# S4D mixing kernel: transposes of x in queues of their own, measured durations in the planner, shared buffers and one merged product

## The chip, the cores and the metric

The kernel runs on one core of a Trainium2 chip. The metric is the time of one execution on the device in microseconds (us), the median of several runs. The core has five engines with programs of their own: TensorE (PE in the profile, with its weight loads as PEld), VectorE (DVE), ScalarE (ACT), GpSimd (POOL) and SyncE (SP), which issues nearly all DMAs here.

## The reference

Sequence length L is 2048, the model width D 640, the hidden width 1728, and the state size N 128. All data is fp32.

```python
x = A_u                                                       # [1, 2048, 640]
g = sigmoid((x * gate_w).sum(-1, keepdims=True))
# A: S4D. A = -exp(log_A_real) + i A_imag, dt = exp(log_dt), C = (C_real + i C_imag) dt
P = exp((A * dt[:, None])[:, :, None] * pos)                  # [640, 128, 2048], pos = 0..2047
K = 2 * einsum("dn,dnl->dl", C, P).real                       # one filter of 2048 taps per channel
a = irfft(rfft(x^T, 2 L) * rfft(K, 2 L))[..., :L]^T + x * D_skip
# B: feed-forward
b = relu(x @ w1) @ w2
return g * a + (1 - g) * b
```

## The kernel before, in words

Three kinds of work share the core, and a planner interleaves them.

*Feed-forward* (`feed_forward`). The hidden width is cut into 14 tiles of 128, done in three passes of 5, 5 and 4 tiles; each matmul operand is split into a high and a low fp32r part (names ending in `h` and `l`), and three products stand for one. Pass 0 goes through eight blocks `g` of 256 rows. Block g is loaded (`load_x`, tile `xu`), transposed on PE (`trans`, in three thirds of two, two and one chunk of 128 columns, into a PSUM bank: `pk` for every block but the first), copied by ACT as the high part and subtracted by DVE as the low part (both into the tile `xx`, which has room for two blocks, ring `xhl`), and stored to DRAM for the later passes (`xt`). `hidden` multiplies it with w1, ACT and DVE make the split relu (`hh`, `hl`), and `sums` multiplies with w2 into partial sums `q` that are stored in DRAM (`part`) and loaded again by the next pass. Passes 1 and 2 take blocks in pairs (`wide`, 512 columns). All of these PE steps stand in one in-order queue, `ff`, with the transposes of block g + 1 between the hidden products of block g.

*Generation of the taps* (`params`, `ssm`). After a chain of parameter steps on DVE, 40 units of 16 channels each are made: `phases` (PE into bank `pg`, ACT takes the whole turns into `cs`, DVE the fraction into `sn`), `exponents` (PE into `px` and `pe`, ACT takes exponentials `mg`, 64 coarse ones per channel, and `me`, 32 fine ones, then sine and cosine in place in `sn` and `cs`), `factors` (five DVE products; the first half of the 64 columns of `sn` and `cs` is the fine table, the second half the coarse one), and per two units `taps` (256 small matmuls into bank `pk`, the same ring as the transposes of x, then a DVE transpose, tile `kt`, and stores to DRAM, `kd`).

*Convolution* (`conv`). Five blocks of 128 channels go through a two-step transform (`stage1` for filter and input, `stage2` with the products of the spectra, `inv2`, `relay`, `inv1`). All its matmuls write PSUM tiles `pc` of two banks each from the ring `psc` of three. `inv1` works in two halves `j` and two parts `q`: two 128x512 products in the first bank of a tile, then four ACT multiplications with the gate into `yo`, which are joined with the partial sums of pass 1 or stored for pass 2.

*The planner.* Nothing is written in loops over engines. Every step is a `Task` with an engine, a queue, a duration, dependencies, buffers that it takes and uses, and a rank; `Plan.run` simulates the engines greedily in time (the lowest rank among the steps that are ready, each queue in order) and issues the instructions in the order so found, which is then the order of each engine's program. `LAG`, `CHANGE` (extra time when an engine changes mode: `f` full matmuls, `c` and `c1` convolution, `t` taps), `FETCH` and the DMA rate are its model of the chip; they carry no wait into the program but decide the order. A DMA step has a size `kb`, and the planner lets all DMAs run one after the other at 270 KB/us (230 in the first 12 us):

```python
if t.kb:
    dma = max(dma, start + min(t.dur, 0.62) + 0.5) + t.kb / (230 if start < 12 else 270)
    t.end = max(dma, start + t.dur) + 1.1
```

The line in the profile for nearly all instructions is L314, that of the helper `Pinned`, so groups are told apart by tiles.

Of the kernel before, what the change touches and what calls it, by code (L numbers as in the profile page):

```python
# [10 lines left out]
F32 = mybir.dt.float32  # L11
# [43 lines left out]
S2P = 2  # L55
RLR = 2
S4A = 0
POOLED = 0
PA = 3
PL = 2.5  # L60
YO = 5
# [80 lines left out]
class Plan:  # L142
# [5 lines left out]
    FETCH = 2.4  # L148
    BUSY = 2.6
    SLACK = .8  # L150
    BURST, GATHER, PATIENCE = ('c', 'c1'), 2, 3

    def __init__(self):
# [68 lines left out]
    def run(self):  # L222
# [3 lines left out]
        while True:  # L226
# [39 lines left out]
                break  # L266
            _, e, t, start = best
            change = self.CHANGE.get(e, 0) if t.mode is not None and mode.get(e) not in (None, t.mode) else 0
            if e == 'PE' and t.mode != 'f':
                since = start + t.dur  # L270
            if t.mode is not None:
# [16 lines left out]
                self.free[e] += 0.25 * min(max(self.free['POOL'] - start, 0), t.dur)  # L288
            t.end = self.free[e] + t.lag
            if t.kb:  # L290
                dma = max(dma, start + min(t.dur, 0.62) + 0.5) + t.kb / (230 if start < 12 else 270)
                t.end = max(dma, start + t.dur) + 1.1
            for b in (*t.take, *t.use):
                b.left -= 1
                b.free = max(b.free, t.end)
# [49 lines left out]
class Kernel:  # L345
# [30 lines left out]
    def feed_forward(self):  # L376
# [109 lines left out]
        def trans(g, third, src):  # L486
            s_, ld = src
            bank = ('pk', 'px', 'pg')[0 if g else third]
            b_ = tok(bank)
            if third == 0:  # L490
                xtok[0, g] = tok('xhl')
            x_ = xtok[0, g]
            k0, kn = 2 * third, min(2, NT - 2 * third)

            def pe():
                ps = self.psg.tile([128, 2 if bank == 'pk' else 4, 256], F32, name=bank)
                ps = st['xb', g, third] = ps[:, :2]
# [13 lines left out]
            a = A('PE', 'ff', 0.22 * kn, pe, [ld], take=[b_], use=[s_], mode='f')  # L511
            b = A('ACT', 'ff', 0.12 + 0.2 * kn, high, [a], take=[x_] if third == 0 else (),
                  use=[b_] if third == 0 else [b_, x_], rank=0)
            c = A('DVE', 'ff', 0.08 + 0.27 * kn, low, [b], use=[b_, x_], rank=0)
            X.setdefault((0, g), []).extend((b, c))
            self.x_read.append(a)

            def store():
                for l, x in enumerate(st['x', g]):
                    D_.dma_start(sc['xt'][g][l], x.bitcast(F32))  # L520
            if third == 2:
                if g:
# [88 lines left out]
        def wide(p, P, f):  # L611
# [34 lines left out]
            ts = [A('PE', 'ff', 0.69, pe(k), [*wt, *xd_], take=() if k else [b_], use=[w_, *xs_] + ([b_] if k else []),  # L646
                    mode='f', n=3) for k in range(NT)]
            a = A('ACT', 'ff', 0.52, high, [*ts, *(self.zs if p == 1 and f > 1 else ())], take=[h_], use=[b_], rank=0)
            b = A('DVE', 'ff', 0.62, low, [a], use=[b_, h_], rank=0)
# [141 lines left out]
        for p, n in enumerate(PARTS):  # L791
# [3 lines left out]
            for k, g in enumerate(order):  # L795
# [28 lines left out]
                if not last:  # L824
                    es = [sums(p, g, j, q_, qld) for j in range(4)]

                    def store(p=p, g=g):
                        D_.dma_start(sc['part'][p % 2][g], st['q', g])
                    done[p, g] = A('SP', 'st', 0.62, store, es, use=[q_], kb=640, rank=6, late=True)
                    continue  # L830
                if k % 2 == 0 and k < 6:
                    paced = [x for i in order[k + 2:k + 4] for x in X[p, i]]
# [179 lines left out]
    def ssm(self, C=16):  # L1012
# [52 lines left out]
        def phases(c):  # L1065
            p_, s_ = tok('pg'), tok('sc')
            rd, r_ = rows[c]

            def pe():
                p = self.psg.tile([128, 4, 256], F32, name="pg")  # L1070
                pf = p.rearrange("p d j -> p (d j)")
                st['pg'] = pf.rearrange("p (d j) -> p d j", j=64)
                for h in range(2):
                    x = slice(h * 512, h * 512 + 512)
                    self.E.matmul(pf[:, x], R[c], self.tg[:, x], start=True, stop=True)

            def whole():
                st['sc', c] = [st['gp'].tile([128, C, 64], F32, name=k, bufs=5) for k in ("sn", "cs")]
                S.copy(I(st['sc', c][1]), st['pg'])
            a = visit[c, 1] = A('PE', None, 0.5, pe, [rd, opened, *self.tg_done], take=[p_], use=[r_], rank=GPR, mode='f')  # L1080
            b = acts[c, 0] = A('ACT', None, 0.97, whole, [a], take=[s_], use=[p_], rank=2)
            d = A('DVE', 'g1', 1.14, lambda: V.tensor_sub(st['sc', c][0], st['pg'], I(st['sc', c][1])), [b],
                  use=[p_, s_], rank=G1R)
            e = A('DVE', 'g1', 0.62, lambda: V.tensor_scalar(I(st['sc', c][1]), I(st['sc', c][0]), 0x7fffffff, None,
                                                             op0=ALU.bitwise_and), [d], use=[s_], rank=G1R, port=True)
            tasks[c] = dict(s=s_, abs=e)

        def exponents(c):
# [13 lines left out]
            def exps(k):  # L1102
# [8 lines left out]
            a = visit[c, 2] = A('PE', None, 0.7, pe, [rd, opened, *self.tg_done], take=[p_], use=[r_], rank=GPR, mode='f')  # L1111
# [10 lines left out]
        def factors(c):  # L1122
# [3 lines left out]
            def part(k):  # L1126
                def go():
# [5 lines left out]
                    elif k == 1:  # L1133
                        V.tensor_mul(st['G', c][:, :, 32:], mg[:, :, 32:], sn[:, :, 32:])
                    elif k == 2:
                        m = mg.rearrange("p d (h j) -> p d h j", h=2)
                        V.tensor_mul(m, m, cs[:, :, None, 32:].to_broadcast([128, C, 2, 32]))
                    elif k == 3:
                        V.tensor_mul(cs[:, :, :32], me, cs[:, :, :32])
                    else:  # L1140
                        (P if POOLED else V).tensor_mul(sn[:, :, :32], me, sn[:, :, :32])
                return go
            (ex, me), (sn, cs) = w['exps'], w['trig']
            fs = []
            for k, dep in enumerate(((ex, sn), (ex, sn), (ex, cs), (me, cs), (me, sn))):
                if k == 4 and POOLED:
                    fs.append(A('POOL', 'g2', 1.5, part(k), dep, use=[w['s'], w['m']]))
                    continue
                fs.append(A('DVE', 'g4', 1.2 if k == 2 else 0.62, part(k), dep, take=[g_] if k == 0 else (),
                            use=[w['s'], w['m']] + ([g_] if k == 1 else []), rank=G4R, port=True))  # L1150
            w.update(G=g_, f=fs)

# [1 line left out]
        def taps(p):  # L1154
# [23 lines left out]
            a = visit[p, 0] = A('PE', None, 2.0, pe, [*w[0]['f'], *w[1]['f']], take=[b_], use=us, rank=GTR, mode='t', n=128)  # L1178
# [32 lines left out]
    def conv(self, C=128):  # L1211
# [182 lines left out]
        def inv1(i, j, dep):  # L1394
            last = i == n - 1
            for q in range(2):
                b_, b0 = tok('psc'), j * 8 + q * 4
                ns = min(max(2 * sum(c <= i for c in CG) - b0, 0), 4)
                y_ = tok('yo') if ns or not last else None
                g_, first = None, False  # L1400
# [4 lines left out]
                def pe(q=q, b0=b0):  # L1405
                    py = st['p4', i, b0] = self.psc.tile([128, 2, 4, C], F32, name="pc")
                    for h in range(2):
                        self.E.matmul(py[h * 64:h * 64 + 64, 0].rearrange("p b c -> p (b c)"), st['tw'],
                                      st['K', i][:, h * 4 + b0 // 4], start=True, stop=True)

                def copy(q=q, b0=b0, ns=ns, y_=y_, first=first):
# [4 lines left out]
                    x = st['p4', i, b0][:, 0].rearrange("p b c -> p (b c)").rearrange("p (c b) -> p b c", b=4)  # L1416
# [124 lines left out]
```

## Time and profile before

| | before |
|---|---|
| median of 3 runs | 644.29 us (642.56 to 644.78) |
| profiled execution | 642.35 us |
| its span, first to last instruction | 640.6 us |
| PE, PEld busy | 617.3, 503.0 us |
| DVE, ACT, POOL busy | 508.5, 402.1, 93.9 us |
| DMA | 107.78 MB, mean 168 GB/s |
| granted TensorE clock | 1.00 |

The profile is of one execution. A stretch in which PE is busy all the time is one that PE bounds, if its work is needed there; a wait names the instruction that stood still and what released it. An engine's idle time costs nothing where another engine sets the pace.

### The profile page before, as it was taken

To read this page: it belongs to the slowest core of one execution; us is meant where nothing else is said; L and a number is where in the kernel's file an instruction comes from. 1 tells how busy PE (TensorE), PEld (TensorE's weight loads), DVE (VectorE), ACT (ScalarE), POOL (GpSimd) and SP (SyncE) were. 2 spreads that over 40 slices of the span, in tenths; PEclk is the share of its full clock that TensorE was granted. 3 is DMA by queue.
4 is the path that set the end of the run, shared out by engine and by line. 5 is a ranking of instruction groups with operands and counts; after the bars stand their busy time and mean duration, and the time that the engine had idled before them with its cause. 6 is when DMAs were issued, how large, how long until landed. Compare 5 with 4: busy or idle time off the path is not lost.

```text
span 640.6 us, 19212 instructions
## 1 busy us (share of the span) xinstructions
PE 617.3 (96%) x8236; PEld 503.0 (79%) x8236; DVE 508.5 (79%) x818; ACT 402.1 (63%) x603; POOL 93.9 (15%) x134
## 2 busy tenths in 40 slices
PE   7989999899999899999999999999999999999897
PEld 6989998798898798898898898665565556756577
DVE  4889936989999999998999999768579753966542
ACT  5557439999999988988978985113443424432550
POOL 0000000000000000000000000024151531713633
PEclk9999999999999999999999999999999999999999
DMA  9974774333456734373454225794406558156355
GB/s 256 326 236 147 221 229 165 105 125 112 136 167 210 255 122 144 122 242 117 129 198 154 79 80 176 258 315 132 144 3 215 185 164 263 53 158 188 102 166 133
DMA packets 76176, 107.78 MB, mean 168 GB/s; under 512 B 7610, under 2 KB 58682, under 8 KB 75195
## 3 DMA queue, kind: packets, MB, share of 16 engines
q1 hardware_dynamic: 75930, 106.14, 53.2%
q8 instruction: 65, 1.06, 0.7%
q10 hardware_dynamic: 160, 0.41, 0.3%
q14 instruction: 21, 0.16, 0.1%
HBM read 67.47 MB, written 44.30 MB: 174 GB/s over the span
## 4 chain that ended last, share of the span: by engine, by line
PE 56%; DVE 5%; DMA 2%; ACT 2%; issue 1%; SPq 1%; DVEq 0%; ACTq 0%
PE pf L314 35%; PE pc L314 13%; PE pk L314 4%; DVE ku L314 3%; PE pg L314 2%; PE px L314 2%; DMA part<-q 1%; ACT ku L314 1%; PE pe L314 1%; DMA out_dram<-yo 1%; SPq L314 1%; DVE sn L314 1%; ACT cs L314 0%; DVE q L314 0%; ACT q L314 0%
## 5 line engine op out<-in xcount | busy, mean ns | idle before, releaser
L314 PE MATMUL pf<-xx,w1h 128*128 128x256 f32 (+1 forms) x760 | 184.2, 339 | 0.4 <-DVE xx L314 0.3
L314 PEld LDWEIGHTS pf<-xx,w1h 128*128 128x128 f32 x760 | 125.2, 189 | 22.8 <-issue 7.3
L314 PE MATMUL pf<-xx,w1l 128*128 128x512 f32 (+1 forms) x340 | 115.7, 340 | 0.0
L314 PE MATMUL pf<-w2h,hh 128*128 128x320 f32 x288 | 89.7, 315 | 2.4 <-DVE hl L314 1.5
L314 PE MATMUL pf<-w2l,hh 128*128 128x320 f32 x288 | 87.8, 309 | 0.0
L314 ACT COPY ku<-pc 128x512 f32<-128x512 f32 (+1 forms) x60 | 43.8, 761 | 68.2 <-PE pc L314 56.7
L314 PE MATMUL pf<-w2h,hl 128*128 128x320 f32 x256 | 73.3, 312 | 0.0
L314 PEld LDWEIGHTS pf<-xx,w1l 128*128 128x128 f32 x340 | 64.3, 189 | 7.6 <-DVE w1l L314 0.2
L314 POOL TENSOR_TENSOR kt<-kt,dsk 128x8 f32<-128x8 f32 x20 | 10.3, 515 | 392.7 <-DVE kt L314 377.8
L314 POOL TENSOR_TENSOR ku<-ku 128x256 f32<-128x256 f32 x80 | 56.2, 737 | 55.3 <-DVE ku L314 49.1
L314 DVE TENSOR_TENSOR ku<-pc,ku 128x512 f32<-128x512 f32 x80 | 52.6, 684 | 12.5 <-ACT ku L314 11.3
L314 DVE STREAM_TRANSPOSE ku<-pc 128x512 f32<-128x512 f32 x80 | 50.2, 683 | 13.7 <-PE pc L314 13.7
L314 PEld LDWEIGHTS pf<-w2h,hh 128*128 128x128 f32 x288 | 54.1, 188 | 7.7 <-issue 3.7
L314 DVE TENSOR_TENSOR sn<-pg,cs 128x1024 f32<-128x1024 f32 x40 | 48.7, 1217 | 7.5 <-ACT cs L314 7.5
L314 PEld LDWEIGHTS pf<-w2l,hh 128*128 128x128 f32 x288 | 54.1, 188 | 0.6
L314 ACT ACT_TABLE_LOAD x42 | 53.9, 1283 | 0.7
L314 ACT CAST cs<-pg 128x1024 int32<-128x1024 f32 x40 | 40.3, 1008 | 21.2 <-PE pg L314 21.0
L314 DVE TENSOR_TENSOR mg<-mg,cs 128x1024 f32<-128x1024 f32 x40 | 48.9, 1222 | 1.3
L314 PEld LDWEIGHTS pf<-w2h,hl 128*128 128x128 f32 x256 | 46.4, 188 | 3.5 <-issue 2.9
L314 PE MATMUL pc<-ku,tm 64*32 64x256 f32 x1280 | 42.2, 392 | 3.6 <-DVE ku L314 2.4
L314 ACT ACTIVATE cs<-cs,half_pi 128x1024 f32<-128x1024 f32 x40 | 45.6, 1140 | 0.0
L314 ACT ACTIVATE hh<-pf 128x512 fp32r<-128x512 f32 (+1 forms) x40 | 20.5, 513 | 39.4 <-PE pf L314 39.4
(170 smaller groups left out, 1232.5 us busy)
## 6 DMA issues: line engine op xcount, KB each, us to landing
xx<-xt SPq DMA_DIRECT2D x24, 640.0 KB, 6.8
xt<-xx SPq DMA_DIRECT2D x16, 640.0 KB, 3.9
part<-q SPq DMA_DIRECT2D x16, 640.0 KB, 3.4
q<-part SPq DMA_DIRECT2D x16, 640.0 KB, 5.3
ws<-in_B_w_dram SPq DMA_DIRECT2D x20, 320.0 KB, 5.5
kd<-kt SPq DMA_DIRECT2D x80, 64.0 KB, 1.8
ub<-in_A_u_dram SPq DMA_DIRECT2D x10, 512.0 KB, 4.7
xu<-ub SPq DMA_DIRECT2D x5, 1024.0 KB, 6.2
```

The source lines that it names most:

```text
L314: self._last = self._tc.keep_in_program_order(f(*a, **k))
```

## The change

It has five parts, all in one file.

- `trans`: the PE, ACT and DVE steps of x's transposes stand in queues `xp` of their own in place of `ff`, on PE at rank 4.5 (the rank of `ff` is 5; the lower goes first).
- `phases`, `factors`, `taps`: sine and cosine of a unit are two halves of one tile `sc`, and the two fine products with `me` become one DVE instruction over both (with `me` broadcast). The unused variant on POOL is deleted.
- `inv1`: the two parts `q` of a half share one PSUM tile, one bank each; the tile is freed after the second part's ACT copies.
- `Plan.run`: DMA steps have a rate by queue, a step of several DMAs is modelled as several, and the latencies are 1.15 and 1.27 us. A change of PE to or from taps costs half as much.
- Durations: `wide` 0.69 to 0.681 us, `phases` 0.5 to 0.46, `exponents` 0.7 to 0.69, `taps` 2.0 to 1.83, the store of partial sums from 640 to 310 KB.

```diff
+    RATE = dict(x=330, q=287, st=320, yq=200, y4=260, mx=297, cu=215, kd=231, ub=401, xt=485, rows=697, prm=215, tab=340, tab0=171)
...
+            if e == 'PE' and 't' in (t.mode, mode.get(e)):
+                change /= 2
...
             if t.kb:
-                dma = max(dma, start + min(t.dur, 0.62) + 0.5) + t.kb / (230 if start < 12 else 270)
-                t.end = max(dma, start + t.dur) + 1.1
+                m = max(1, round(t.dur / 0.625))
+                for j in range(m):
+                    dma = max(dma, start + 0.62 * j + 1.15) + t.kb / m / self.RATE.get(t.q, 250)
+                t.end = max(dma, start + t.dur) + 1.27
...
-            a = A('PE', 'ff', 0.22 * kn, pe, [ld], take=[b_], use=[s_], mode='f')
-            b = A('ACT', 'ff', 0.12 + 0.2 * kn, high, [a], take=[x_] if third == 0 else (),
+            a = A('PE', 'xp', 0.22 * kn, pe, [ld], take=[b_], use=[s_], rank=4.5, mode='f')
+            b = A('ACT', 'xp', 0.12 + 0.2 * kn, high, [a], take=[x_] if third == 0 else (),
                   use=[b_] if third == 0 else [b_, x_], rank=0)
-            c = A('DVE', 'ff', 0.08 + 0.27 * kn, low, [b], use=[b_, x_], rank=0)
+            c = A('DVE', 'xp', 0.08 + 0.27 * kn, low, [b], use=[b_, x_], rank=0)
...
-                    done[p, g] = A('SP', 'st', 0.62, store, es, use=[q_], kb=640, rank=6, late=True)
+                    done[p, g] = A('SP', 'st', 0.62, store, es, use=[q_], kb=310, rank=6, late=True)
...
-                st['sc', c] = [st['gp'].tile([128, C, 64], F32, name=k, bufs=5) for k in ("sn", "cs")]
+                t = st['tr', c] = st['gp'].tile([128, 2, C, 64], F32, name="sc", bufs=5)
+                st['sc', c] = [t[:, k] for k in range(2)]
...
-                    elif k == 3:
-                        V.tensor_mul(cs[:, :, :32], me, cs[:, :, :32])
                     else:
-                        (P if POOLED else V).tensor_mul(sn[:, :, :32], me, sn[:, :, :32])
+                        t = st.pop(('tr', c))[:, :, :, :32]
+                        V.tensor_mul(t, me[:, None].to_broadcast([128, 2, C, 32]), t)
...
-                fs.append(A('DVE', 'g4', 1.2 if k == 2 else 0.62, part(k), dep, take=[g_] if k == 0 else (),
+                fs.append(A('DVE', 'g4', 1.2 if k > 1 else 0.62, part(k), dep, take=[g_] if k == 0 else (),
...
-                b_, b0 = tok('psc'), j * 8 + q * 4
+                b0 = j * 8 + q * 4
+                b_ = b_ if q else tok('psc')
...
-                    py = st['p4', i, b0] = self.psc.tile([128, 2, 4, C], F32, name="pc")
+                    if not q:
+                        st['p4', i, j] = self.psc.tile([128, 2, 4, C], F32, name="pc")
+                    py = st['p4', i, j]
                     for h in range(2):
-                        self.E.matmul(py[h * 64:h * 64 + 64, 0].rearrange("p b c -> p (b c)"), st['tw'],
+                        self.E.matmul(py[h * 64:h * 64 + 64, q].rearrange("p b c -> p (b c)"), st['tw'],
                                       st['K', i][:, h * 4 + b0 // 4], start=True, stop=True)
...
-                a = A('PE', 's4', 0.87, pe, [*dep, tw], take=[b_], use=[K[i]], rank=S4R, mode='c1')
+                a = A('PE', 's4', 0.87, pe, [*dep, tw], take=() if q else [b_], use=[K[i]] + ([b_] if q else []), rank=S4R, mode='c1')
```

More of the change, by code (lines that the diff above doesn't have):

```diff
@@ L57 @@
 S4A = 0
-POOLED = 0
 PA = 3
@@ L645, in wide @@
             wt, w_ = W[p, f, 0]
-            ts = [A('PE', 'ff', 0.69, pe(k), [*wt, *xd_], take=() if k else [b_], use=[w_, *xs_] + ([b_] if k else []),
+            ts = [A('PE', 'ff', 0.681, pe(k), [*wt, *xd_], take=() if k else [b_], use=[w_, *xs_] + ([b_] if k else []),
                     mode='f', n=3) for k in range(NT)]
@@ L1077, in whole @@
             def whole():
-                st['sc', c] = [st['gp'].tile([128, C, 64], F32, name=k, bufs=5) for k in ("sn", "cs")]
+                t = st['tr', c] = st['gp'].tile([128, 2, C, 64], F32, name="sc", bufs=5)
+                st['sc', c] = [t[:, k] for k in range(2)]
                 S.copy(I(st['sc', c][1]), st['pg'])
-            a = visit[c, 1] = A('PE', None, 0.5, pe, [rd, opened, *self.tg_done], take=[p_], use=[r_], rank=GPR, mode='f')
+            a = visit[c, 1] = A('PE', None, 0.46, pe, [rd, opened, *self.tg_done], take=[p_], use=[r_], rank=GPR, mode='f')
             b = acts[c, 0] = A('ACT', None, 0.97, whole, [a], take=[s_], use=[p_], rank=2)
@@ L1110, in exps @@
                 return go
-            a = visit[c, 2] = A('PE', None, 0.7, pe, [rd, opened, *self.tg_done], take=[p_], use=[r_], rank=GPR, mode='f')
+            a = visit[c, 2] = A('PE', None, 0.69, pe, [rd, opened, *self.tg_done], take=[p_], use=[r_], rank=GPR, mode='f')
             b = acts[c, 1] = A('ACT', None, 0.52, exps(0), [a], take=[m_], use=[p_], rank=2, mode='exp')
@@ L1144, in factors @@
             fs = []
[L1145 to L1148, printed above, removed]
-                fs.append(A('DVE', 'g4', 1.2 if k == 2 else 0.62, part(k), dep, take=[g_] if k == 0 else (),
+            for k, dep in enumerate(((ex, sn), (ex, sn), (ex, cs), (me, cs, sn))):
+                fs.append(A('DVE', 'g4', 1.2 if k > 1 else 0.62, part(k), dep, take=[g_] if k == 0 else (),
                             use=[w['s'], w['m']] + ([g_] if k == 1 else []), rank=G4R, port=True))
@@ L1177, in out @@
                                  kt[32 * j:32 * j + 32].rearrange("p h q b -> p h (q b)"))
-            a = visit[p, 0] = A('PE', None, 2.0, pe, [*w[0]['f'], *w[1]['f']], take=[b_], use=us, rank=GTR, mode='t', n=128)
+            a = visit[p, 0] = A('PE', None, 1.83, pe, [*w[0]['f'], *w[1]['f']], take=[b_], use=us, rank=GTR, mode='t', n=128)
             b = A('DVE', 'g5', 0.65, turn, [a], take=[k_], use=[b_], rank=G5R)
@@ L1403, in inv1, with pe, copy @@
                     g_ = self.gy_tok = self.gy_tok or tok('K')
-                def pe(q=q, b0=b0):
-                    py = st['p4', i, b0] = self.psc.tile([128, 2, 4, C], F32, name="pc")
+                def pe(q=q, b0=b0, j=j):
+                    if not q:
+                        st['p4', i, j] = self.psc.tile([128, 2, 4, C], F32, name="pc")
+                    py = st['p4', i, j]
                     for h in range(2):
-                        self.E.matmul(py[h * 64:h * 64 + 64, 0].rearrange("p b c -> p (b c)"), st['tw'],
+                        self.E.matmul(py[h * 64:h * 64 + 64, q].rearrange("p b c -> p (b c)"), st['tw'],
                                       st['K', i][:, h * 4 + b0 // 4], start=True, stop=True)
-                def copy(q=q, b0=b0, ns=ns, y_=y_, first=first):
+                def copy(q=q, b0=b0, ns=ns, y_=y_, first=first, j=j):
                     if first:
@@ L1415, in copy @@
                         st['yo', i, b0] = self.pr.tile([128, 4, C], F32, name="yo", bufs=YO)
-                    x = st['p4', i, b0][:, 0].rearrange("p b c -> p (b c)").rearrange("p (c b) -> p b c", b=4)
+                    x = st['p4', i, j][:, q].rearrange("p b c -> p (b c)").rearrange("p (c b) -> p b c", b=4)
                     for b in range(4):
```

## The prediction

> **What bounds the kernel now.** I read the busy shares first, then the stretches, then the list of waits, then the chain.
>
> ```profile
> span 640.6 us, 19212 instructions
> PE 617.3 (96%) x8236; PEld 503.0 (79%) x8236; DVE 508.5 (79%) x818; ACT 402.1 (63%) x603; POOL 93.9 (15%) x134
> 0.00:20.00 20.00, 15.87 (x109) 14.74 (x110) 11.09 (x20) 11.84 (x22) 0.87 (x7) 1.00 0.96 265
> 20.00:100.00 80.00, 76.15 (x568) 74.30 (x568) 61.24 (x133) 42.40 (x100) 0.00 (x0) 1.00 0.69 217
> 100.00:220.00 120.00, 113.54 (x1516) 103.34 (x1515) 111.76 (x178) 113.10 (x147) 3.62 (x7) 1.00 0.50 163
> 220.00:400.00 180.00, 179.88 (x2374) 159.68 (x2373) 170.29 (x241) 151.28 (x170) 6.46 (x12) 1.00 0.45 143
> 400.00:580.00 180.00, 177.72 (x2943) 110.27 (x2942) 127.87 (x208) 61.30 (x116) 55.73 (x76) 1.00 0.55 174
> 580.00:640.60 60.60, 54.12 (x736) 40.69 (x734) 26.20 (x44) 22.21 (x52) 27.25 (x32) 0.99 0.53 140
> ```
>
> The last six rows are stretches: start and end, length, then busy time of PE, of its weight loads, of DVE, ACT and POOL, granted clock, DMA share, GB/s. TensorE (PE) is the bound: 617.3 of 640.6 us, at full clock throughout. Its idle time is 640.6 − 617.3 = 23.3 us, and the rows say where: 4.1 in the first 20 us, 3.85 to 100, 6.5 to 220, 0.1 to 400, 2.3 to 580 and 6.5 in the last 60.6. The change takes no matmul away, so nearly all that it can win on PE lies in those 23.3 us. The chain's last pieces (start, length, what) agree that the end is set by PE's remaining work:
>
> ```profile
> 620.01 3.65 PE pc L314 x16
> 623.67 13.12 PE pf L314 x88
> 636.88 0.55 DVE q L314
> ```
>
> The last matmuls of the convolution (pc) are over at 623.67, and 88 matmuls of the feed-forward (pf) are still queued behind them, 13.1 us. Then come one DVE step and a store. So in this program idle time of PE anywhere before is paid for at the end, and work on other engines is free while PE has something to do.
>
> Now the waits, engine, tile and line, then releaser: total, times, longest.
>
> ```profile
> PEld pk L314 <- DVE xx L314: 6.9, 6, 1.9
> PE pk L314 <- DVE xx L314: 5.6, 5, 1.7
> PE pk L314 <- DMA xu<-in_A_u_dram: 2.3, 2, 1.1
> PE pg L314 <- DVE sn L314: 2.1, 1, 2.1
> PE pf L314 <- DVE hl L314: 1.5, 1, 1.5
> PE pf L314 <- ACT hh L314: 0.9, 1, 0.9
> PE pc L314 <- DVE ku L314: 3.1, 6, 1.7
> ```
>
> The largest is "pk waits for DVE xx": 5.6 us. pk is the one PSUM bank through which x is transposed in pass 0, two chunks of 128 columns at a time, and xx is the residual that DVE takes out of that bank.
>
> **The change, part by part.**
>
> *x's transposes in queues of their own.* In the kernel before they stand in the same in-order queue `ff` as the feed-forward's matmuls. When the third pair finds the bank not yet emptied, PE stops, though the products with the second weights are ready behind it:
>
> ```profile
> 13.47 0.63 PE L314 MATMUL pk<-ident,xu 128*128 128x128 f32 x4 [1.15 <-DMA xu<-in_A_u_dram]
> 13.85 0.49 PE L314 MATMUL pf<-xx,w1h 128*128 128x256 f32 x2
> 40.99 0.44 PE L314 MATMUL pk<-ident,xu 128*128 128x128 f32 x2 [1.74 <-DVE xx L314]
> 41.19 0.39 PE L314 MATMUL pf<-w2h,hh 128*128 128x320 f32 x1
> 117.92 0.32 PE L314 MATMUL pk<-mg,cs 128*32 128x64 f32 x8 [0.81 <-DVE xx L314]
> 124.92 0.44 PE L314 MATMUL pk<-ident,xu 128*128 128x128 f32 x2 [1.42 <-DVE xx L314]
> ```
>
> In the lines at 13.47, 40.99 and 124.92 the work behind the wait needs nothing of it: at 41.19 it is the second product (pf from w2 and hh) of the block before. With `xp` apart, at rank 4.5 against 5, the planner puts a transpose in as soon as x and the bank are there and otherwise goes on with `ff`. Removable are the 5.6 us and the 1.15 us at 13.47, in all 6.75; the other x wait has nothing in front of it and stays. What is late next: the 0.2 us of transposes and the wait together gave ACT and DVE time to bring hh and hl of the last hidden pair before the sums need them. Without that cover the sums can wait as in the two rows of 0.9 and 1.5 us. There are seven blocks with such a cover. Bounds: 0 and 7 × 0.9 = 6.3; I take 1.5 in all, because eight products with older hh stand ahead of the last one's in the first sum (at the planner's 0.147 us each that is 1.2 us of cover by itself). Worth −6.75 + 1.5 = −5.2 us, between −6.75 and −0.5.
>
> *Sine and cosine in one buffer, one product.* Rows by form (count, busy, mean ns):
>
> ```profile
> L314 DVE TENSOR_TENSOR mg<-mg,cs 128x1024 f32<-128x1024 f32 x40 | 48.9, 1222 | 1.3
> L314 DVE TENSOR_TENSOR sn<-me,sn 128x512 f32<-128x512 f32 x40 | 27.3, 682 | 0.0
> L314 DVE TENSOR_TENSOR cs<-me,cs 128x512 f32<-128x512 f32 x40 | 27.3, 682 | 0.0
> ```
>
> Two of 682 ns become one over 1024 columns with a broadcast operand, as mg's product is already: 1222 ns. Saved: 40 × (0.682 + 0.682 − 1.222) = 5.7 us of DVE. It lies in the generation of the taps, which fills the rows up to 400 us, and in 220 to 400 PE has 0.1 us of idle time, so there it is hidden entirely by PE's own work. It can reach PE only through the wait on sn (2.1 us). I take −0.5, bounds −2.1 and 0. The merged product waits for sine and cosine both; the product before it on DVE waits for the cosine, which is the later one, so no wait is added.
> [...]
>
> *Shared PSUM buffer in the inverse stage.* Two 128x512 products per half now share one buffer of the three (both of its banks), where each took a whole one.
>
> ```profile
> 478.47 3.28 PE L314 MATMUL pc<-ku,tw 128*64 128x512 f32 x12
> 481.68 0.73 PE L314 MATMUL pf<-xx,w1h 128*128 128x512 f32 x2
> ```
>
> Twelve of these take 3.21 us to the next start; undisturbed, sixteen take 3.65 (the chain row at 620.01), so twelve take 2.74. The wait for a buffer costs 3.21 − 2.74 = 0.47 us here, and there are five blocks, the last of them undisturbed. I take −0.7 in all, bounds −1.9 (four times 0.47) and +1 (a buffer is now held for two ACT passes, so the next block's first product can be the one that waits).
>
> *Measured durations.* They move no instruction by themselves; they change in which order the planner writes the engines' programs. The clearest misjudgement that the trace shows is a transfer:
>
> ```profile
> 576.53 0.55 SPq L314 DMA_DIRECT2D part<-q  x1
> 583.35 3.49 SPq L314 DMA_DIRECT2D yj<-part  x5
> 586.94 0.54 SPq L314 DMA_DIRECT2D q<-part  x1
> 591.83 0.83 ACT L314 ACTIVATE q<-q,omg 128x640 f32<-128x640 f32 x1 [4.96 <-DMA out_dram<-yo]
> ```
>
> A store of partial sums is issued at 576.53, five loads that need it stand next on SP and start at 583.35, and the q load behind them at 586.94. ACT stands at a multiplication with that q until 591.83, with the convolution's copies queued behind it; the convolution's DVE and PE steps are late in turn (the 3.1 us of pc on ku, most of it here). From its issue to the loads the store took 6.8 us. In the planner's old model this store, 320 KB, lands (0.62 + 0.5 + 320/270 + 1.1) = 3.4 us after its step starts; in the new one (1.24 + 1.15 + 107/320 + 1.27) = 4.0. Both are short of the measured time, and the first figure differs little from the second, so I don't count on this wait going. The order as a whole will be another one. Bounds: −3.1 (the waits of pc on ku gone) and +5 (two waits more like the largest one above, 2.1 us, with its train); I take 0, being nearest to the rows of 220 to 400, where a planned order loses 0.1 us whatever its details.
>
> **Sum.** −5.2 − 0.5 − 0.7 + 0 = −6.4 us. The profiled execution took 642.35 us (640.6 of span and 1.8 around it) and would take 636.0; the median of the three runs is 644.29, 1.9 above it. On the median: 644.3 − 6.4 = 637.9, put as 638.
>
> **Rivals.**
>
> *The bank is held (slower).* The eager transposes take pk early and keep it until ACT may copy, and ACT may copy only when the xx buffer of two blocks before is free, that is after that block's hidden products and its store. The taps use the same bank.
>
> ```profile
> 101.59 1.47 SPq L314 DMA_DIRECT2D xu<-in_A_u_dram  x2
> 123.22 0.28 PE L314 MATMUL pf<-xx,w1l 128*128 128x256 f32 x1
> L314 ACT CAST xx<-pk 128x512 fp32r<-128x512 f32 x15 | 8.7, 581 | 0.4
> L314 DVE TENSOR_TENSOR xx<-pk,xx 128x512 fp32r<-128x512 f32 x15 | 10.3, 684 | 0.6 <-ACT xx L314 0.6
> 231.16 1.92 PE pk L314 x128
> 244.90 1.92 PE pk L314 x128
> ```
>
> The x of the last block is issued at 101.59, so its transpose can take pk before 110, while the hidden products that hold the buffer end at 123.22. The first taps, at 117.92 now, would wait until about 124.6 (0.58 for the copy and 0.68 for the residual after 123.4): 6.7 us. Of such a delay D the generation may get 5.7 back from the merged product. Before it shows at the end, it must also use up the slack there: the convolution's last matmul ends 17 us before the span does and I allow 5 for its copy, add and store, so some 12 us. It decides from D = 12. One turn of the taps more lost, 13.7 us by the last two rows, gives D = 6.7 + 13.7 = 20.4, less 5.7 is 14.7; without that relief (DVE not being what then limits) 20.4 − 12 = 8.4 us too late: with 1.5 us of the transposes' gain left, 644.3 + 8.4 − 1.5 = 651. For it: a greedy list scheduler doesn't see that it blocks. Against it: after 124.6 all of x is through and pk belongs to the taps alone.
>
> *Nothing measurable.* The order changes, the transposes' waits go, and waits on hh and hl (up to 6.3) or on the convolution take their place: 644. For it: ACT and DVE are at 113 and 112 of 120 us in 100 to 220.
>
> *DVE counts.* If the generation sets the pace rather than PE, the 5.7 us of DVE come on top: 644.3 − 6.4 − 5.2 = 632.7. For it: DVE's 170.29 of 180 and weight loads of only 159.68 in the same row. Against it: PE's 179.88, and 13.1 us of pf left over at the end. [...]
>
> **How the numbers follow.** Forecast (635 to 641 by the bounds of the terms): 0.50. DVE counts: 0.10, about 633. Nothing measurable: 0.16, about 644. Slower, by the held bank or by new waits of the reordered program: 0.24, from 647 to 651. A measurement of this kernel can tell about 0.3% from no change, 1.9 us. Faster: 0.50 + 0.10 = 0.60, same 0.16, slower 0.24. The range is to leave out 2 in 10: below, a twentieth; above, the worse part of the slower case. That gives 632 to 648; the forecast's own range is 635 to 641.
>
> **What would show it.** Right: no wait of pk on DVE xx over 1 us; transposes in the timeline earlier than now and not directly ahead of the sums; PE idle of about 17 us in place of 23.3; 40 DVE rows of about 1222 ns for the merged product and 5 to 6 us less DVE time; the end still a train of pf matmuls. Wrong: taps that start later than 124 and a generation that ends after 405 (bank held); new waits of pf on hh or hl of more than 3 us in all; a chain that ends in pc, ku and yo instead of pf; more idle time than 7 us between 400 and 620.

## The result and the profile after

| | before | after |
|---|---|---|
| median of 22 runs each | 643.40 us (641.84 to 646.45) | 642.63 us (639.40 to 649.51) |
| ratio, 95% interval | | 0.9987 (0.9974 to 0.9999) |
| profiled execution, span | 642.35, 640.6 us | 642.32, 640.5 us |
| PE busy, idle | 617.3, 23.3 us | 621.2, 19.3 us |
| granted TensorE clock | 1.00 | 0.997 |

The ratios here and below leave out two slow executions, one of after's 22 (649.51 us) and one of null_d's 12 (996.03 us at a mean clock of 0.558). The change is worth 0.8 us, 0.13%, which is within the 0.3% taken as no change; 638.0 was forecast. The waits that it aimed at did go. In the profiled executions PE idles 4.0 us less, but PE is busy 3.9 us longer with the same 8236 matmuls.

The head of the page of after, and the same six stretches as were shown of before (start and end, length, busy time of PE, its weight loads, DVE, ACT, POOL, then granted clock, DMA share, GB/s):

```profile
span 640.5 us, 19160 instructions
PE 621.2 (97%) x8236; PEld 505.1 (79%) x8236; DVE 506.1 (79%) x778; ACT 402.3 (63%) x603; POOL 93.5 (15%) x134
0.00:20.00 20.00, 17.58 (x114) 15.93 (x115) 11.10 (x20) 12.04 (x22) 0.87 (x7) 1.00 0.96 265
20.00:100.00 80.00, 78.55 (x585) 76.17 (x583) 64.82 (x139) 44.36 (x102) 0.00 (x0) 1.00 0.74 241
100.00:220.00 120.00, 116.91 (x1539) 106.75 (x1538) 111.20 (x160) 112.05 (x145) 3.48 (x7) 1.00 0.47 152
220.00:400.00 180.00, 178.59 (x2347) 156.43 (x2346) 165.33 (x213) 152.36 (x171) 6.10 (x12) 1.00 0.44 145
400.00:580.00 180.00, 174.00 (x2914) 109.16 (x2917) 126.33 (x205) 59.15 (x113) 56.60 (x77) 0.99 0.56 168
580.00:640.60 60.60, 55.58 (x748) 40.70 (x740) 27.30 (x45) 22.35 (x52) 26.45 (x31) 1.00 0.54 143
```

Up to 220 us PE's idle time is 2.42 + 1.45 + 3.09 = 6.96 us, where it was 14.44: the change wins 7.5 us there. From 220 to 400 it is 1.4 instead of 0.1, from 400 to 580 it is 6.0 instead of 2.3. Five of the 7.5 us are given back in these two stretches; in the last one 1.5 us are won. The waits of after (engine, tile, releaser; total, times, longest):

```profile
PE pk L318 <- DVE xx L318: 0.2, 1, 0.2
PE pk L318 <- DMA xu<-in_A_u_dram: 0.5, 1, 0.5
PE pf L318 <- DVE hl L318: 2.7, 3, 2.0
PE pf L318 <- ACT hh L318: 0.4, 1, 0.4
PE pf L318 <- issue: 2.4, 1, 2.4
```

"pk waits for DVE xx" has gone from 5.6 to 0.2 us, and the wait on hl and hh together rises from 2.4 to 3.1. New is the row "issue": 2.4 us in which PE stood with nothing to wait for that the profile shows (its cause was not shown; more in the last section). The timeline of PE has it (start, length, matmul, count; in brackets the idle time before):

```profile
476.15 0.31 PE L318 MATMUL pf<-w2h,hl 128*128 128x320 f32 x1
476.30 0.31 PE L318 MATMUL pf<-w2h,hh 128*128 128x320 f32 x1
476.68 2.10 PE L318 MATMUL pc<-ku,tn 32*64 32x128 f32 x128
478.96 0.31 PE L318 MATMUL pf<-w2h,w1h 128*128 128x320 f32 x1
481.63 0.42 PE L318 MATMUL pf<-w2l,w1h 128*128 128x320 f32 x1 [2.37 <-issue]
481.86 0.47 PE L318 MATMUL pf<-w2h,w1l 128*128 128x320 f32 x1
482.12 0.47 PE L318 MATMUL pf<-w2h,w2h 128*128 128x320 f32 x1
```

Before the pause the 320-column products start 0.15 us apart (476.15, 476.30); after it 0.26 us (481.86, 482.12). The same moments in stretches of 2 us show why; the column behind the five engines is the granted clock:

```profile
478.00:480.00 2.00, 1.27 (x58) 0.98 (x43) 1.81 (x4) 1.21 (x2) 0.00 (x0) 1.00 0.51 196
480.00:482.00 2.00, 0.37 (x2) 0.36 (x2) 0.00 (x0) 0.81 (x1) 0.00 (x0) 0.78 0.01 1
482.00:484.00 2.00, 2.00 (x9) 1.79 (x7) 0.55 (x1) 0.00 (x0) 0.00 (x0) 0.50 0.03 8
484.00:486.00 2.00, 2.00 (x121) 1.88 (x126) 0.00 (x0) 0.00 (x0) 0.00 (x0) 0.87 0.95 174
```

From 481.1 us, 1.9 us into this standing, the clock is 0.5 for 0.9 + 2 + 0.5 = 3.4 us, and the products' starts lie nearly twice as far apart: by estimate, half of the 3.4 us, the pause costs up to another 1.7 us, booked as busy time. But before's clock falls too in most of its runs: of the 98 runs of before made beside the experiments below 60 have a mean clock of 0.997 or less. Over all 98 it is 0.9976, over after's runs 0.9973. The execution of before that was profiled, at 1.00, is one of its better ones. The chain's last pieces are what they were, PE's remaining feed-forward work:

```profile
619.48 3.58 PE pc L318 x16
623.06 13.70 PE pf L318 x92
636.85 0.55 DVE q L318
```

### The profile page after: what moved, and what is told of

Same layout as the page of the kernel before. It is cut to its first block, busy times and chain, and to the rows that moved or that the text cites. A ratio compares the mean times of both kernels' runs of the same rounds, so it can differ in the third digit from the quotient of the medians.

```text
span 640.5 us, 19160 instructions
## 1 busy us (share of the span) xinstructions
PE 621.2 (97%) x8236; PEld 505.1 (79%) x8236; DVE 506.1 (79%) x778; ACT 402.3 (63%) x603; POOL 93.5 (15%) x134
## 4 chain that ended last, share of the span: by engine, by line
PE 76%; DVE 9%; DMA 7%; ACT 3%; issue 2%; SPq 1%; POOL 0%; ACTq 0%; DVEq 0%
PE pf L318 50%; PE pc L318 13%; PE pk L318 6%; PE pg L318 3%; PE px L318 3%; DMA ck<-kd 2%; SPq L318 1%; DMA part<-q 1%; PE pe L318 1%; DVE ku L318 1%; DVE sc L318 1%; DMA q<-part 1%; DVE hl L318 1%; DMA wq<-in_B_w_dram 1%; DMA ps<-hl 1%
## 5 line engine op out<-in xcount | busy, mean ns | idle before, releaser
L318 PE MATMUL pf<-w2h,hl 128*128 128x320 f32 x256 | 75.1, 315 | 0.6 <-DVE hl L318 0.6
L318 ACT CAST sc<-pg 128x1024 int32<-128x1024 f32 x40 | 40.4, 1010 | 25.8 <-PE pg L318 25.5
L318 DVE TENSOR_TENSOR sc<-pg,sc 128x1024 f32<-128x1024 f32 x40 | 48.6, 1214 | 4.9 <-ACT sc L318 4.9
L318 DVE TENSOR_TENSOR mg<-mg,sc 128x1024 f32<-128x1024 f32 x40 | 48.9, 1222 | 1.5
L318 DVE TENSOR_TENSOR sc<-me,sc 128x1024 f32<-128x1024 f32 x40 | 48.6, 1216 | 0.0
L318 ACT ACTIVATE sc<-sc,half_pi 128x1024 f32<-128x1024 f32 x40 | 45.6, 1139 | 0.0
```

The source lines that it names most:

```text
L318: self._last = self._tc.keep_in_program_order(f(*a, **k))
```

## The experiments

Sixteen kernels besides before and after can be set side by side in one ledger. For the profiled execution of each: span, PE's idle time (span less PE busy), the time at which the granted clock was 0.5 ("half"), and the rest, PE busy less half of that time. The ratio is that of the medians against before, measured on the same chip.

| kernel | ratio (95%) | span | idle | half | rest |
|---|---|---|---|---|---|
| before | 1 | 640.6 | 23.3 | 0 | 617.3 |
| after | 0.9987 (0.9974 to 0.9999) | 640.5 | 19.3 | 3.4 | 619.5 |
| xp_only | 0.9985 (0.9961 to 1.0008) | 640.2 | 18.9 | 6.8 | 617.8 |
| mul_only | 1.0123 (1.0087 to 1.0158) | 647.2 | 26.1 | 10.2 | 616.0 |
| psc_only | 1.0017 (0.9997 to 1.0038) | 641.6 | 25.1 | 0 | 616.6 |
| plan_only | 1.0231 (1.0195 to 1.0266) | 654.5 | 29.2 | 10.2 | 620.2 |
| mul_frozen | 1.0025 (1.0003 to 1.0047) | 640.2 | 20.9 | 3.4 | 617.6 |
| null_b | 0.9958 (0.9935 to 0.9982) | 639.1 | 20.7 | 3.4 | 616.7 |
| gap_short | 1.0026 (1.0004 to 1.0049) | 643.4 | 23.7 | 3.4 | 618.0 |
| gap_long | 1.0118 (1.0079 to 1.0156) | 652.1 | 28.9 | 13.7 | 616.4 |
| rate_only | 1.0269 (1.0222 to 1.0316) | 663.0 | 35.4 | 13.7 | 620.8 |
| dur_only | 1.0063 (1.0033 to 1.0094) | 642.7 | 22.7 | 6.8 | 616.6 |
| no_rate | 1.0314 (1.0280 to 1.0349) | 661.1 | 32.9 | 27.3 | 614.5 |
| no_xp | 1.0123 (1.0096 to 1.0149) | 649.1 | 27.4 | 10.2 | 616.6 |
| null_c | 0.9966 (0.9937 to 0.9994) | 637.8 | 18.5 | 0 | 619.4 |
| null_d | 0.9994 (0.9971 to 1.0016) | 642.0 | 19.6 | 6.8 | 619.0 |
| xp_w | 1.0205 (1.0156 to 1.0254) | 657.2 | 28.2 | 17.1 | 620.4 |
| xp_fill | 0.9964 (0.9945 to 0.9984) | 642.1 | 20.1 | 6.8 | 618.6 |

Half clock in the last 3 us, after PE's last work, is not counted. The rest stays within 614.5 to 620.8, while idle time plus half of the half-clock time runs from 18.5 to 46.6 us. So these two explain the large differences; a spread of 6 us in the rest is more than most of the small ones.

**The parts alone.** `xp_only` is before with the diff's three lines of `trans`; `mul_only` with its lines of `phases` and `factors`; `psc_only` with its lines of `inv1`; `plan_only` with the DMA model, the durations and the halved change time.

> The kernel before with one part of the change: x's transposes in their own queues. If the waits decide (the pass-0 waits go and nothing takes their place): 4 to 5 us faster than before, 638.5 to 639.5, pk's waits on DVE xx under 1 us, PE idle about 18.5. If any reordering only deals the waits anew: within 2 us of before, with idle time of PE that reappears between 100 and 600 us. If the bank is held: taps later than 124 us and slower.

> The kernel before with sine and cosine in one tile and the one merged product. If PE bounds the generation: within 1 us of before, DVE busy 5.7 us less. If DVE bounds it: 4 to 6 us faster. If reordering alone decides: anything within 3 us, with other waits in the convolution.

> The kernel before with the shared PSUM tile of the inverse stage alone; nothing before 470 us can differ. By the waits: 0.5 to 1.5 us faster, and weight loads of pc wait less for ACT ku (14.6 us before). If reordering decides: the last 170 us come out 2 us either way.

> The kernel before with the planner's DMA rates, latencies and durations alone; the instructions are the same and only their order differs. If the new durations are what costs (the changed kernel lost in 400 to 600 us what pass 0 won): 3 to 5 us slower than before, PE idle over 5 us between 400 and 580, SP waits on part<-q. If they are neutral: within 1 us. If they are better: 2 to 4 us faster, and the cause of the missing gain lies elsewhere.

Measured: −0.15, +1.23, +0.17 and +2.31%, together +3.6%, where the whole change gave −0.13%. The parts don't add. In xp_only the wait of the transposes goes as it does in after, and PE's idle time falls by 4.4 us, but the time does not follow. A wait for the taps' sine, 2.1 us long in before as well, is now followed by half clock (xp_only: the wait of the transposes, the matmul behind the sine wait in the timeline, and two stretches):

```profile
PE pk L314 <- DVE xx L314: 0.5, 1, 0.5
212.19 0.73 PE L314 MATMUL pg<-tg,PS 128*128 128x512 f32 x2 [2.09 <-DVE sn L314]
210.00:212.00 2.00, 0.10 (x1) 0.00 (x0) 2.00 (x3) 1.84 (x3) 0.00 (x0) 1.00 1.01 405
214.00:216.00 2.00, 1.18 (x36) 0.94 (x40) 1.94 (x3) 2.00 (x4) 0.00 (x0) 0.50 0.78 271
```

This holds over the runs: the mean clock of xp_only's twelve is 0.9928, that of the 23 of before beside them 0.9975. The difference, 0.47% of 640 us, is 3.0 us, and with the 1.0 us measured it makes up nearly the 4.4 us of idle time.

psc_only shows no gain (+1.1 us, interval −0.2 to +2.4; 0.5 to 1.5 us faster was expected), though the wait of weight loads that the sharing aims at is shorter. In before and in psc_only (list of waits):

```profile
PEld pc L314 <- ACT ku L314: 14.6, 20, 1.9
```

```profile
PEld pc L314 <- ACT ku L314: 6.4, 11, 1.7
```

mul_only and plan_only are slower by pauses in other places of their new orders and by half clock. In mul_only PE stands 5.0 us from 216.2 and then runs at half clock:

```profile
PE pg L314 <- DVE sc L314: 5.0, 1, 5.0
222.00:225.00 3.00, 2.09 (x9) 1.05 (x7) 2.96 (x4) 2.25 (x3) 0.00 (x0) 0.50 0.43 130
```

**The same product without a new order, and a change of order without content.** A part alone also makes the planner write another order. `mul_frozen` keeps before's order exactly: of the two planned products the first issues nothing and the second does both.

```diff
                     elif k == 3:
-                        V.tensor_mul(cs[:, :, :32], me, cs[:, :, :32])
+                        pass
                     else:
-                        (P if POOLED else V).tensor_mul(sn[:, :, :32], me, sn[:, :, :32])
+                        t = st.pop(('tr', c))[:, :, :, :32]
+                        V.tensor_mul(t, me[:, None].to_broadcast([128, 2, C, 32]), t)
```

`null_b` does the opposite:

```diff
-A('PE', 'ff', 0.69, pe(k)
+A('PE', 'ff', 0.689, pe(k)
```

This is the planner's duration of `wide`. No instruction is another one, but 1304 lines of PE's program stand elsewhere.

> The kernel before with the merged product, but written in the order of the kernel before: the planner is still told of two products, the first issues nothing and the second is the merged one, so every other instruction stands where it stood. If the merged product alone slowed the variant that had it planned: about 650 again. If the new order did, through PE's idle time and the halved clock behind it: 642 to 643, DVE busy about 2.4 us less, clock 1.00 as in the kernel before. If DVE bounds the generation: 3 us or more faster than before.

> The kernel before with one planned duration (the wide product's) at 0.689 instead of 0.69 us; 1304 lines of PE's order differ, all from the second half of the program, and no instruction. If reordering by itself deals time out: up to 4 us off before, either way. If only meaningful edits move the time: within 0.5 us.

The merged product in the old order wins nothing (+1.6 us, interval +0.2 to +3.0); the rest of mul_only's 1.2%, some 1.0%, goes with its new order. And the meaningless null_b is 0.42% faster than before (0.18 to 0.65), three times what the whole change gave.

**Pauses of PE, by themselves.** Before with a chain ahead of the sums of block 2: a matmul, an ACT copy, one (`gap_short`) or six (`gap_long`) additions on POOL, and a matmul that needs them. Their result is unused.

```diff
+                    if p == 0 and g == 2:
+                        def gap():
+                            x = self.psg.tile([128, 16, 32], F32, name="pe").rearrange("p a b -> p (a b)")
+                            self.E.matmul(x[:, :128], self.ident, self.ident, start=True, stop=True)
+                            S.copy(self.scr, x[:, :128])
+                            for _ in range(6):
+                                P.tensor_add(self.scr, self.scr, self.ident)
+                            self.E.matmul(x[:, 128:256], self.ident, self.scr, start=True, stop=True)
+                        A('PE', 'ff', 0, gap, mode='f', n=1e-6)
```

> The kernel before with a pause put into PE after the sums of block 2 (near 69 us): a small matmul, an ACT copy of it, one POOL addition, a small matmul that reads it; the planner's order is kept. The pause should last 1.2 to 1.8 us. [...] If any pause halves the clock: +3 us or more.

> The same with six POOL additions in the pause, 3 to 4.5 us. By the clock theory: the granted clock falls to 0.5 some 2 to 4 us after the pause begins and stays there for 3.4 us or a multiple; time + the pause + 1.7 us for each 3.4. If the clock has nothing to do with pauses: time + the pause alone, and clock 1.00.

gap_short, then gap_long; the matmul behind the pause, and the stretches after it:

```profile
70.87 0.49 PE L314 MATMUL pe<-scr,ident 128*128 128x128 f32 x2 [1.25 <-POOL scr L314]
72.00:74.00 2.00, 2.00 (x19) 2.00 (x18) 0.23 (x1) 0.00 (x0) 0.00 (x0) 1.00 1.06 399
```

```profile
73.33 0.80 PE L314 MATMUL pe<-scr,ident 128*128 128x128 f32 x2 [4.83 <-POOL scr L314]
72.00:74.00 2.00, 0.67 (x3) 0.67 (x4) 0.00 (x0) 0.00 (x0) 1.12 (x3) 0.50 1.01 373
74.00:76.00 2.00, 2.00 (x11) 2.00 (x11) 0.00 (x0) 0.00 (x0) 0.00 (x0) 0.50 0.20 67
```

In these executions a pause of 1.25 us leaves the clock behind it at 1.00; it costs 1.7 us (interval 0.3 to 3.2). One of 4.83 us, longer than the 3 to 4.5 expected, goes with half clock from 70.8 to 77.7, 6.8 us (the clock is 0.71, 0.50, 0.50 and 0.58 in the four stretches of 2 us from 70 to 78), and costs 7.6 us (5.1 to 10.0); at most 4.8 + 6.8/2 = 8.2 was to be expected with the clock's share, 4.8 without it. So this long pause cost more than its length. Between lies the wait for sine near 212 us. In before, which was shown at full clock, and in mul_frozen:

```profile
213.73 0.73 PE L314 MATMUL pg<-tg,PS 128*128 128x512 f32 x2 [2.11 <-DVE sn L314]
212.00:216.00 4.00, 2.12 (x41) 1.46 (x45) 3.97 (x6) 3.97 (x4) 0.00 (x0) 1.00 1.00 366
```

```profile
214.45 1.22 PE L314 MATMUL pg<-tg,PS 128*128 128x512 f32 x2 [2.32 <-DVE sc L314]
212.00:216.00 4.00, 1.68 (x5) 1.26 (x5) 3.97 (x5) 3.97 (x5) 0.00 (x0) 0.81 1.01 375
```

2.11 us did not lower the clock, 2.32 us did, and xp_only's 2.09 us did too. So length alone does not decide; what does was not shown. In the ledger the half-clock time comes in multiples of about 3.4 us (3.4, 6.8, 10.2, 13.7), and the one piece in after's trace is 3.4 us long by the rows shown above.

The price shows in runs of one and the same program: of before's 98 runs beside the experiments the 38 with a mean clock of 0.999 or more have a median of 642.12, the 60 at 0.997 or less 643.87, 1.75 us more. One piece at half clock as long as that in after's trace, 3.4 us, would by estimate make it 1.7.

**Which part of the planner's model.** `rate_only` has plan_only's DMA model alone, `dur_only` its durations and change times. `no_rate` and `no_xp` take one part away from the whole change: the DMA model, and the queues `xp`.

> The kernel before with the new DMA model alone (rates by queue, latencies, the size of the stored partial sums); PE's planned durations as before. If the DMA rates are what made the variant with all planner numbers 15 us slower: 650 or more, with PE waits behind loads. If that loss is a bad draw of the order with halved clock behind it: anything from 640 to 650, and the time goes with PE's idle time plus half of the time at clock 0.5.

> The kernel before with the planned durations of PE alone (wide, phases, exponents, taps, the change to taps). If the shorter PE durations are what made the variant slower (the planner then thinks PE fast and DVE late, and PE waits for sn): 650 or more, with waits of pg on DVE sn over 3 us. If a draw of the order: 640 to 650, as PE's idle time and the halved clock have it.

> The changed kernel without the new DMA model. If the parts add up: the DMA model cost 16.5 us alone, so this would be 626. If each set of edits deals an order of its own: 639 to 652, with the time following idle time plus half of the time at clock 0.5.

> The changed kernel with the transposes back in ff. If the parts add up: 0.7 us slower than the changed kernel (the transposes alone gave 0.15%). By the waits: 4 to 6 us slower, with pk waiting 5 to 7 us for DVE xx again. If a draw: anything from 640 to 660.

Alone, the DMA model costs 2.7%; taken out of the whole change, it costs 3.3% to be without it. Its sign depends on what stands beside it, so "the DMA model is worth so much" has no answer. Both times, 659.2 us and 663.6 us, lie outside what was expected of a draw (640 to 650 and 639 to 652); rate_only's time fits "650 or more", but its longest waits are not behind loads. dur_only is 0.63% slower (0.33 to 0.94), 4.1 us, and its mean clock over twelve runs, 0.9927 against 0.9977 in before's runs beside it, makes up 3.2 us of that. Without its queues the change is 1.2% slower than before: the transposes' wait is back, 8.7 us where 5 to 7 were expected (no_xp), and the slow orders each have long waits of their own (rate_only; no_rate with the stretch it lies in):

```profile
PE pk L319 <- DVE xx L319: 8.7, 7, 2.6
```

```profile
PE pk L317 <- DVE xx L317: 7.0, 5, 2.6
PE pc L317 <- issue: 4.1, 2, 2.9
```

```profile
PE pg L316 <- DVE sc L316: 10.1, 4, 5.6
220.00:400.00 180.00, 172.64 (x2286) 150.86 (x2287) 162.44 (x206) 147.54 (x163) 6.12 (x12) 0.94 0.39 127
```

In no_rate the taps' waits leave PE idle for 7.4 us of a stretch in which before idled 0.1, at a mean clock of 0.94.

**Nulls of after, and two tries to do better.** `null_c` and `null_d` are after with 0.681 for `wide` written as 0.682 and 0.680. `xp_w` is xp_only with the split of the weights on ACT and DVE ahead of equals (`rank=1` to `rank=0.9` in its two steps). `xp_fill` is xp_only with seven products into an unused bank ahead of the phases of unit 16, where PE waits for sine; the planner does not know of them, so the order stays.

```diff
+                if c == 16:
+                    k = self.psg.tile([128, 2 * Q, 64], F32, name="pk").rearrange("p a b -> p (a b)")
+                    for _ in range(7):
+                        self.E.matmul(k, R[c], self.tg[:, :512], start=True, stop=True)
```

> The changed kernel with the wide product's planned duration 0.682 in place of 0.681; 101 lines of PE's order differ. If the changed kernel's time is one draw among many: up to 3 us off the changed kernel's 642.6, either way; without the pause of 2.4 us near 479 and the halved clock behind it, 638 to 640. If its time is a property of the edits: 642 to 643.

> The changed kernel with the wide product's planned duration 0.680 in place of 0.681 us, a second meaningless step beside it. With 0.681 at 0.9987 and 0.682 at 0.9966 of before: if such steps deal out a few us, this one lies anywhere from 637 to 650; if the changed kernel sits in a flat place, 640 to 643.

> The transposes in their own queues, and the split of loaded weights at rank 0.9 in place of 1 on ACT and DVE, so that pass 1's second weights come ahead of the generation's DVE steps: PE's wait near 210 us (pg on DVE sn, 2.3 us, with 6.8 us at half clock behind it in the variant with the transposes alone) should go. By the clock theory: 3.4 us of halved clock and 2 us of wait less, 637 to 639, clock 1.00 from 200 to 230. If the transposes bring nothing: 642 to 643.

> The variant with the transposes alone, with seven extra 128x512 products (1.6 us, their result unused) in front of the one generation step at which PE waits 2.1 us for sn near 210 us; planner and order are kept, and no wait is taken away: PE is busy during it instead. By the clock theory: clock 1.00 from 200 to 230, and 2.5 to 3.5 us faster than the transposes alone, so 638.5 to 639.7, although PE does more. If the halved clock has another cause: unchanged, 642, with 6.8 us at 0.5.

The two nulls land 0.21% below and 0.07% above after; with intervals of some 0.3% neither is shown to differ from it. In null_c the row "issue" of PE pf is there again, 1.9 us in two waits, the longest 1.5, and the ledger has no half clock. xp_w was meant as an improvement, to 637 to 639 us, and costs 2%, with 17.1 us at half clock. In xp_fill the wait is filled, and the clock stays full where xp_only's was 0.50:

```profile
211.86 1.80 PE L314 MATMUL pk<-tg,PS 128*128 128x512 f32 x7
214.00:216.00 2.00, 1.67 (x9) 1.00 (x9) 1.97 (x4) 1.99 (x3) 0.00 (x0) 1.00 1.01 411
```

In this execution it fell elsewhere, 6.8 us in all. Over 12 runs each the median of the mean clock is 0.9965 with the seven products and 0.9925 without, which at 640 us is 2.6 us; xp_only at a median clock of 0.9925 had none of its runs above 0.997. The time, 641.0 us where 638.5 to 639.7 was expected, is 0.36% below before (0.16 to 0.55). Against xp_only it is 0.21% or 1.35 us less, with an interval of some 0.3% by the two ratios, so that the gain over xp_only alone is not shown. null_b (0.9958), xp_fill (0.9964) and null_c (0.9966) beat before and, by their medians, after; their intervals overlap with one another and with after's (0.9974 to 0.9999), so none is shown to be the best.

## Why the prediction was wrong

*Transposes in own queues: the mechanism came as forecast, its size at the end didn't.* The wait on xx fell by 5.4 us, that on x's load by 1.8 (forecast for both: 6.75 removable), new waits on hl and hh cost 0.7 where 1.5 was allowed. The last transpose starts at 125.6 us instead of 150.2; the tile's matmuls in after and in before (count; shortest, median, longest in ns; first and last start):

```profile
L318 PE MATMUL pk<-ident,xu x74: 269/272/331, 6.6 to 125.6; 128*128 128x128 f32 x74
L318 PE MATMUL pk<-mg,sc x1280: 218/219/244, 118.8 to 403.5; 128*32 128x64 f32 x183
```

```profile
L314 PE MATMUL pk<-ident,xu x74: 270/273/330, 6.8 to 150.2; 128*128 128x128 f32 x74
L314 PE MATMUL pk<-mg,cs x1280: 219/219/243, 117.9 to 403.0; 128*32 128x64 f32 x183
```

The chain still ends in pf. Of the marks named, idle time was to be about 17 us and is 19.3, because 5 of the 7.5 us won come back as pauses elsewhere. More than 7 us of it between 400 and 620 was named as a mark of a wrong forecast, and it came: 7.2 us, where before has 4.9. Alone the part is worth 1.0 us (interval −0.5 to 2.5), not 5.2: idle time falls by 4.4 us, and the lower clock takes 3.0 of them.

*The term that failed: "Measured durations: 0".* This term put the loss of the whole new order at nothing, because a planned order loses 0.1 us in 220 to 400 "whatever its details". In after that stretch loses 1.4 us and the next one, to 580, 6.0 instead of 2.3: the 5.0 us given back, the largest of them the pause at 479 us (2.4), a wait on `q` (1.2) and waits on `sc` (1.2). xp_only, with the transposes alone, idles 1.9 us in 220 to 580, so they did not bring this. The same lines alone cost 2.3%, 14.9 us, far outside −3.1 to +5; yet without the DMA model the change is 3.3% slower, and in no_rate 220 to 400 loses 7.4 us. The details were the matter. What makes one order bad and another good was not found: the ledger says where the time is (pauses, half clock), not which decision of the planner put it there.

*The assumption that failed beside it: PE's busy time is fixed, "at full clock throughout".* The sum counted idle time only. The row of before at 1.00 bore that out for one execution, but that execution was a lucky one: 60 of before's 98 runs have a mean clock of 0.997 or less. In the transposes alone this is what hid the gain. In after it is not: over the runs its mean clock is before's. Of PE's 3.9 us more of busy time in after's profile, up to 1.7 are the piece at half clock. The other 2.2 us aren't settled.

So of the 5.6 us between the forecast gain and the measured one, 2.4 are idle time that was not won (19.3 in place of 16.9) and 2.2 the unsettled busy time. The last 1.0 can't be placed; the interval of the measured gain, 0.1 to 1.7 us, is wider than that.

*Merged product: −0.5 forecast, nothing found.* The saving of DVE was also too large. Rows of before and of mul_only, neighbours on DVE:

```profile
207.71 0.69 DVE L314 TENSOR_TENSOR cs<-me,cs 128x512 f32<-128x512 f32 x1
208.32 0.69 DVE L314 TENSOR_TENSOR sn<-me,sn 128x512 f32<-128x512 f32 x1
```

```profile
217.68 1.23 DVE L314 TENSOR_TENSOR mg<-mg,sc 128x1024 f32<-128x1024 f32 x1
218.82 1.22 DVE L314 TENSOR_TENSOR sc<-me,sc 128x1024 f32<-128x1024 f32 x1
```

A 512-column product has a row of 0.69 us but the next one starts 0.61 us later; with 1024 columns it is 1.23 and 1.14. Neighbouring rows overlap, so two become one for 2 × 0.61 − 1.14 = 0.08 us, not for 0.14: 40 × 0.08 = 3.2 us, and DVE's busy time fell 2.4 us in after (1.6 in mul_frozen), not 5.7.

*Shared PSUM buffer: −0.7 forecast, +1.1 measured alone* (interval −0.2 to +2.4), at the upper bound, +1, and not shown to be beyond it.

*The rivals.* "Bank is held" is refuted: by the rows above the taps start at 118.8 us (117.9 before) and their last products at 403.5 (403.0). "DVE counts" isn't borne out: DVE's 2.4 us less show nowhere. "Nothing measurable" at 644 is how it came out, but not by its mechanism: the waits on hl and hh that it named grew by 0.7 us, a tenth of what was won. Pauses behind 220 us took most.

## What to carry over

In a program whose order a planner writes, every edit is also a draw of a new order: a null edit (a duration changed by 0.001 us) moved the time by as much as 0.42%, and a gain smaller than that says nothing about the edit. Where a part is to be judged, freeze the order and change the content alone, as mul_frozen does. And count a wait of TensorE not by its length alone: with a wait of 2.09 us in xp_only and one of 4.83 us in gap_long the clock fell to 0.5 for 6.8 us, with one of 2.11 us in before it stayed at 1.00. A wait removed in one place was worth little where another one then cost clock (xp_only: 4.4 us of idle time less, 1.0 us of time). One profiled execution does not show this; the mean clock over the runs does.

## What the chip showed that was not expected

- Half clock after short pauses: in the profiled executions 1.25 us did not bring it, 2.09 to 2.37 us sometimes did, 4.83 us gave 6.8 us of it. What decides was not shown. Filling such a pause with products that nobody uses goes with a mean clock of 0.9965 in place of 0.9925 (medians of xp_fill and xp_only).
- PE stood 2.37 us at 479 us in after, and in rate_only 4.1 us in two such waits (the row on "issue" above), with nothing to wait for that the profile shows. In after the pause came two products (at 478.71 and 478.96 us) behind 128 short products issued within 2.1 us; before has such 128 products at the same time (476.44 us), with twelve 128x512 products behind them, and no pause. The cause was not shown: no run was made to find it.
